# A fused attention and MLP kernel on one core: the order of every engine planned by a list scheduler, and later scores computed on two 64-row TensorE tiles

## The chip, the cores and the metric

The kernel runs on 1 core of a Trainium2 chip. The time is the device time of one execution in microseconds (us), taken as a median over runs. The engines are written as the profile names them: PE is TensorE (PEld is its weight load, which overlaps), DVE is VectorE, ACT is ScalarE, POOL is GpSimd, SP is SyncE. "The profile" is one recorded execution. Its span is the time from the first to the last instruction, 1.7 to 1.9 us shorter than the device time. Of the kernel before, one execution in three of the four groups was slow (345.9, 345.4 and 346.0 us); the medians and ranges below contain it, the ratios leave it out.

## The reference

Block-sparse attention, then a residual MLP with token mixing. The inputs are 4 batches, 8 heads, 768 tokens and 64 dimensions a head; the MLP is 512 wide with 2048 hidden units.

```python
scores = (q @ k.T) / 8                      # per batch and head, 768 x 768
scores = where(mask, scores, -1e9)          # 32x32 blocks: window, first and last, 3 sampled ones
attn   = softmax(scores);  x = attn @ v     # heads side by side: x is 768 x 512 per batch
a1 = alpha1 * x + beta1
u  = x + lam * (w_tok @ a1)                 # token mixing, 768 x 768
a2 = alpha2 * u + beta2
out = u + lam * (relu(a2 @ w_ch1) @ w_ch2)  # 512 -> 2048 -> 512
```

The q and k inputs are normal draws times 0.1, so all scores are close to 0.

## The kernel before

Heads are taken in 16 pairs. A pair's 2 x 768 x 768 transposed scores are cut into 9 units of 1024 columns. For each unit, PE makes the scores into one of two score buffers (`sps`, two PSUM banks each), ACT takes the exp into `eT` (float16), and PE multiplies that with v (PV). The mask rides in the contraction: 64 rows of q and k plus 24 rows that hold the block mask.

```python
def emit_qk(b, n, u):
    sps = ps.tile([P, UN], FP, name="sps", tag="sps", bufs=2)
    ...
        nc.tensor.matmul(sps[:, ...w columns],
            kx[h][0:KC, ts(jt, P)],          # KC = 64 + 24 rows: k and block indicator
            qx[h][0:KC, c : c + w], ...)     # q and mask bias
    eT = wk.tile([P, UN], F16, name="eT", tag="eT", bufs=5)
    nc.scalar.activation(eT[:], sps[:], AF.Exp, bias=EXPB, scale=SCALE)
```

The order of instructions is set by hand, by a loop over the 144 units. Each step issues the scores of unit i, the PV matmuls of unit i-2, one piece of token mixing, and as many MLP matmuls as a "credit" in estimated nanoseconds allows. The engines keep that order.

```python
for i in range(len(units) + LAG):
    emit_qk(b, n, u)
    ...                                      # loads, casts, transposes at fixed steps
    credit += work[ph] / NS
    if i >= NS: spent += filler(C1 if i % 2 else C2)     # MLP groups
    if i >= LAG: ... pv_tile(...)                         # PV of unit i - 2
    if mixq: spent += mix_next(i)                         # token mixing
    if i >= NS: spent += filler(1e9)
```

PSUM: two score buffers, two general banks (`mm`), one bank for PV (`ops`), one for the second MLP product (`cp`). From pair 7 on, q and k are transposed by DMA instead of PE. The MLP of a batch can start only when all four pairs of that batch have been mixed, so batch 0 has no MLP work to fill PE with.

The softmax here doesn't subtract the row's maximum and nothing guards it: scores larger than these inputs give would overflow.

## Time and profile before

| | before |
|---|---|
| device time, median (range), 3 executions | 342.8 us (340.6 to 345.9) |
| span | 339.7 us |
| PE, DVE, ACT busy | 319.1, 177.7, 192.0 us |
| first MLP matmul | 72.0 us |

First the page. Its part 1 gives each engine's busy time with its share of the span and its instruction count; part 2 gives the busy tenths in 40 slices, with the granted PE clock and the load of the DMA engines; part 4 is the chain of waits by engine.

```profile
PE 319.1 (94%) x3216; PEld 205.9 (61%) x3248; DVE 177.7 (52%) x359; ACT 192.0 (57%) x230; POOL 45.0 (13%) x71
...
PE   6898988689989999999999999999999999999995
...
DVE  4399989577774646365544545364543727100011
...
PEclk9799999899999999999999999999999999999999
DMA  7999999614292949295954525252420021000011
...
PE 80%; DVE 13%; issue 3%; DMA 2%; ACT 1%; POOL 0%; ACTq 0%; DVEq 0%; POOLq 0%
```

PE is the chain. The weak part is the first quarter, where DVE and the DMA engines are full. The windows view shows the same per 20 us. Its columns are the stretch, its length, the busy time of PE, PEld, DVE, ACT and POOL (with instruction counts), the clock, the DMA share and GB/s.

```profile
20.00:40.00 20.00, 18.19 (x283) 14.48 (x281) 18.74 (x41) 17.16 (x18) 11.73 (x18) 1.00 1.15 234
40.00:60.00 20.00, 17.40 (x260) 13.38 (x259) 17.71 (x45) 14.34 (x16) 7.13 (x11) 1.00 1.27 204
60.00:80.00 20.00, 16.50 (x241) 12.43 (x242) 12.88 (x29) 10.34 (x12) 1.41 (x2) 0.91 0.30 44
...
160.00:180.00 20.00, 19.89 (x196) 12.72 (x197) 9.98 (x20) 11.60 (x14) 2.86 (x4) 1.00 0.64 107
```

"Busy" overstates PE, because the recorded durations of successive matmuls overlap: a 512-column one lasts some 384 ns, and the next starts 216 ns after it. What counts is the distance from start to start. In the timeline of PE (start, length, operation, count) one score unit runs from 162.61 to 163.05, so 1024 columns take 0.44 us; four 384-column matmuls take 0.65 us.

```profile
161.72 0.41 PE L357 MATMUL ops<-vext,eT 128*128 128x65 f16 x8
161.96 0.81 PE L454 MATMUL mm<-uT,w1b 128*128 128x384 bf16 x4
162.61 0.60 PE L336 MATMUL sps<-qx,kx 88*128 88x512 bf16 x3
```

The measured spacings (56 ns for 128 columns, 109 for 256, 162 for 384, 216 for 512, about 30 for 65) lie on a line, 0.417 ns a column plus 2.5, with a floor for short ones (25 ns for 1 column). Whatever a distance has beyond that line is called a gap below; time lost to a slower clock counts as a gap too. "PE work" is the sum of spacings over all matmuls. For this kernel it is 308.2 us. (32 of its 3248 matmul records are missing from the trace; the sum counts them, and the 6 us that they take are not counted as gaps.)

### The profile page before, as it was taken

The numbers are of one execution on the slowest core, as the hardware profiler recorded it, in microseconds if no ns is written. First come the engines' busy times: TensorE is split into PE (matmuls) and PEld (weight loads), VectorE is DVE, ScalarE is ACT, GpSimd is POOL, SyncE is SP. The second block draws the span as 40 slices with busy tenths as digits, with TensorE's granted clock in tenths as the row PEclk, the third lists the DMA queues.
The fourth block names the chain that finished last, engine by engine and source line by source line (L and its number), as shares of the span: only waits on it lengthen the run. The fifth ranks groups of instructions, "written<-read, shape, count | busy, mean of one in ns | idle before, by whom it ended". The sixth has DMA issues, their size and how long they took to land.

```text
span 339.7 us, 7549 instructions
## 1 busy us (share of the span) xinstructions
PE 319.1 (94%) x3216; PEld 205.9 (61%) x3248; DVE 177.7 (52%) x359; ACT 192.0 (57%) x230; POOL 45.0 (13%) x71
## 2 busy tenths in 40 slices
PE   6898988689989999999999999999999999999995
PEld 3586766567665757566566756567566655555542
DVE  4399989577774646365544545364543727100011
ACT  5698786365756565566556564475656550373420
POOL 7466332101201111010100000000000000000000
PEclk9799999899999999999999999999999999999999
DMA  7999999614292949295954525252420021000011
GB/s 155 192 254 221 206 207 202 91 25 59 42 136 46 162 89 172 57 132 62 154 87 76 72 56 125 56 94 54 79 71 32 2 56 62 33 31 31 33 62 62
DMA packets 57685, 32.61 MB, mean 96 GB/s; under 512 B 38924, under 2 KB 53428, under 8 KB 57652
## 3 DMA queue, kind: packets, MB, share of 16 engines
q0 software_dynamic: 15984, 15.47, 28.9%
q1 hardware_dynamic: 41344, 16.42, 23.2%
q8 instruction: 25, 0.41, 0.5%
q10 hardware_dynamic: 324, 0.23, 0.2%
q14 instruction: 8, 0.07, 0.1%
HBM read 30.90 MB, written 6.29 MB: 109 GB/s over the span
## 4 chain that ended last, share of the span: by engine, by line
PE 80%; DVE 13%; issue 3%; DMA 2%; ACT 1%; POOL 0%; ACTq 0%; DVEq 0%; POOLq 0%
PE cp L486 21%; PE mm L454 19%; PE sps L336 14%; PE mm L409 8%; PE ops L357 8%; PE sps L454 3%; PE ops L486 3%; DMA v<-in_v_dram 2%; DVE a1p L396 2%; DVE x_sb L374 2%; DVE ot L495 1%; DVE x_sb L420 1%; DVE kx L297 1%; DVE ub L421 1%; DVE qx L296 1%
## 5 line engine op out<-in xcount | busy, mean ns | idle before, releaser
L345 ACT ACTIVATE eT<-sps 128x1024 f16<-128x1024 f32 x144 | 145.8, 1024 | 87.9 <-PE sps L336 87.2
L454 PE MATMUL mm<-uT,w1b 128*128 128x384 bf16 x444 | 88.3, 325 | 2.0 <-ACT hts L462 1.5
L336 PE MATMUL sps<-qx,kx 88*128 88x512 bf16 (+1 forms) x384 | 87.3, 329 | 0.9 <-ACT eT L345 0.5
L486 PE MATMUL cp<-w2b,hts 128*128 128x512 bf16 x308 | 79.9, 378 | 2.7 <-DVE ot L495 1.0
L357 PEld LDWEIGHTS <-eT 128*128 128x128 f16 x1152 | 53.9, 98 | 28.5 <-DVE x_sb L374 5.2
L454 PEld LDWEIGHTS <-w1b 128*128 128x128 bf16 x512 | 47.9, 97 | 34.5 <-issue 2.5
L486 PEld LDWEIGHTS <-hts 128*128 128x128 bf16 x384 | 36.3, 97 | 37.3 <-issue 2.5
L357 PE MATMUL ops<-vext,eT 128*128 128x65 f16 x1008 | 52.4, 195 | 3.9 <-DVE x_sb L374 2.4
L462 ACT ACTIVATE hts<-mm,b1t 128x384 bf16<-128x384 f32 x64 | 37.1, 579 | 33.1 <-PE mm L454 31.8
L466 DVE TENSOR_SCALAR hts<-mm,b1t 128x384 bf16<-128x384 f32 x47 | 28.9, 615 | 40.3 <-PE mm L454 34.4
L336 PEld LDWEIGHTS <-kx 88*128 88x128 bf16 x384 | 32.5, 98 | 14.5 <-issue 0.7
L409 PE MATMUL mm<-a1p,wtokT 128*128 128x128 bf16 x576 | 39.3, 219 | 1.4 <-DVE kx L297 1.1
L495 DVE TENSOR_TENSOR ot<-x_sb,cp 128x512 f32<-128x512 f32 x21 | 14.4, 685 | 44.4 <-PE cp L486 44.2
L409 PEld LDWEIGHTS <-wtokT 128*128 128x128 bf16 x576 | 33.1, 98 | 2.5 <-DVE kx L297 1.2
L420 DVE TENSOR_TENSOR x_sb<-x_sb,mm 128x384 f32<-128x384 f32 (+1 forms) x35 | 18.1, 518 | 24.8 <-PE mm L409 24.4
L185 POOL DMA_DIRECT2D v<-in_v_dram x16 | 11.6, 723 | 84.4 <-DVE vext L320 70.9
L421 DVE TENSOR_TENSOR ub<-x_sb,a_bc 128x384 bf16<-128x384 f32 (+1 forms) x35 | 18.3, 523 | 1.2
L374 DVE TENSOR_TENSOR x_sb<-ops,rcp 128x384 f32<-128x384 f32 x28 | 15.6, 557 | 1.0
L399 DVE TENSOR_TENSOR a1p<-a1p,b_bc 128x768 bf16<-128x768 bf16 x16 | 15.3, 957 | 0.6
L396 DVE TENSOR_TENSOR a1p<-x_sb,a_bc 128x768 bf16<-128x768 f32 x16 | 15.3, 956 | 0.5
L462 ACT ACTIVATE hts<-sps,b1t 128x384 bf16<-128x384 f32 x17 | 9.9, 581 | 9.1 <-PE sps L454 8.6
L185 POOL DMA_DIRECT2D q<-in_q_dram x15 | 10.8, 717 | 32.3 <-DVE relp L288 12.4
(77 smaller groups left out, 155.9 us busy)
## 6 DMA issues: line engine op xcount, KB each, us to landing
out_dram<-ot SPq DMA_DIRECT2D x24, 256.0 KB, 2.0
v<-in_v_dram POOLq DMA_DIRECT2D x16, 192.0 KB, 6.0
q<-in_q_dram POOLq DMA_DIRECT2D x15, 192.0 KB, 6.2
k<-in_k_dram POOLq DMA_DIRECT2D x15, 192.0 KB, 6.5
w1b<-in_moe_w_ch_dram POOLq DMA_DIRECT2D x4, 512.0 KB, 9.9
w2b<-in_moe_w_ch_dram POOLq DMA_DIRECT2D x4, 512.0 KB, 15.2
wtk<-in_moe_w_tok_dram POOLq DMA_DIRECT2D x3, 384.0 KB, 9.6
a_bc<-in_moe_alpha_dram POOLq DMA_DIRECT2D x2, 256.0 KB, 7.9
```

Of the source, the lines that this page charges most:

```text
L185: nc.gpsimd.dma_start(t[:], pair_ap(src, b, n))
L336: nc.tensor.matmul(sps[:, f - u * UN : f - u * UN + w], kx[h][0:KC, ts(jt, P)], qx[h][0:KC, c : c + w], start=True, stop=True,)
L345: nc.scalar.activation(eT[:], sps[:], AF.Exp, bias=EXPB, scale=SCALE)
L357: nc.tensor.matmul(ops[(b, n, a)][:, t * VW : t * VW + D + 1], eTs[(b, n, u)][:, ts(c, P)], vx[:, a, jt, 0 : D + 1], start=(r == 0), stop= ...
L374: nc.vector.tensor_tensor(out=x_sb[:, s0 : s0 + NT, h * D : (h + 1) * D], in0=op[:, :, 0:D], in1=rcp[:].unsqueeze(2).broadcast_to([P, NT, D]),
L396: nc.vector.tensor_tensor(out=a1p[:], in0=x_sb[:, s0 : s0 + NT, cs], in1=bc(a1_bc, NT), op=ALU.mult)
L409: nc.tensor.matmul(tp[:, j, :], wtokT[:, s, ts(m * g + j, P)], a1p[:, s, :], start=(s == 0), stop=(s == NT - 1),)
L421: nc.vector.tensor_tensor(out=ub[:, gs, :], in0=sl, in1=bc(a2_bc, m), op=ALU.mult)
L454: nc.tensor.matmul(hp[:, 0:HS], w1b[:, dk, ts(f, P)], uTs[b][:, dk, ts(hf, HS)], start=(dk == 0), stop=(dk == 3),)
L462: nc.scalar.activation(hts[k][:, f, :], hp[:, 0:HS], AF.Relu, bias=b1t[:, f : f + 1], scale=1.0)
L466: nc.vector.tensor_scalar(out=hts[k][:, f, :], in0=hp[:, 0:HS], scalar1=b1t[:, f : f + 1], scalar2=0.0, op0=ALU.add, op1=ALU.max,)
L486: nc.tensor.matmul(cps[k][:], hts[k][:, nk, ts(m, P)], w2b[:, nk, :], start=(nk == 0), stop=(nk == 15),)
```

## The change

Two things were done at once.

1. A `Plan` class takes every operation with an estimated duration, its dependencies, its buffers and a "due" value, and simulates the engines inside the program. Whenever an engine is free, the ready operation with the smallest due value is emitted. Some copies and ReLUs may go to ACT or DVE, whichever takes them first. PSUM becomes two score buffers plus four general banks (`gb`), and `eT` has 7 buffers instead of 5.
2. From pair 6 on (90 of the 144 units) the scores contract over 64 rows only. Two such matmuls are issued side by side, on rows 0 to 63 and 64 to 127 of PE. The mask no longer fits in the contraction; it becomes a product of `eT` with a 0/1 mask on DVE (the mask table is made once, with 6 small exps). Each pair's q and k are transposed by three DMAs, and two DMAs issued from POOL copy q's halves to the other 64 partitions ("swap").

```diff
+class Plan:
+    def run(self):
+        t = min(self.free.values())
+        while todo:
+            ...                                # release buffers that are done at t
+                for op in todo:
+                    if any(d.vis is None or d.vis > t for d in op.deps): continue
+                    ...                        # buffers there? engine free?
+                        if self.free[e] <= t and (e not in best or op.due < best[e][0].due):
+                            best[e] = (op, o)
+                op, (e, occ, vis) = min(best.values(), key=lambda x: x[0].due)
+                ...
+                self.free[e] = t + occ
+                op.emit(op)
...
-    for i in range(len(units) + LAG):
-        ...
-            emit_qk(b, n, u)
...
+    def emit_qk_rows(pi, u, key):
+        ...
+            for r in range(2):
+                rows = slice(r * D, (r + 1) * D)
+                o = r * 512 + f % 512
+                nc.tensor.matmul(
+                    spsT[sl(key)][:, o : o + w],
+                    kd[i][rows, h, g, :],
+                    qx2[i][rows, h, c : c + w],
...
+    def emit_mult(op, i):
+        e = eTt[sl(("eT", i))][:].rearrange("p (r c) -> p r c", r=2)
+        x = i % NU * 512 % HF
+        nc.vector.tensor_tensor(out=e, in0=e, in1=msk[:, :, x : x + 512], op=ALU.mult)
...
+        batch = [i] if pi < T0 else [i, i + 1]      # T0 = 6: two tiled units in one PE group
+        occ = 437 if pi < T0 else 640
```

## The prediction

> **What bounds the kernel now.** TensorE: PE 319.1 us of a 339.7 us span (94%, the page), DVE 52%, ACT 57%; the chain of waits is 80% PE. From start to start in the timeline a matmul costs 56 ns (128 columns), 109 (256), 162 (384), 216-220 (512), about 30 (65). Times the counts that is 308 us of PE work, so only some 31 us are gaps: 7 in the first 20 us, 15 from 20 to 100, about 0.5 in each later 20, 4 after the last matmul. The windows agree: PE 16.5-18.6 of each 20 us from 20 to 100, 19.3-19.9 from 100 to 320. The early gaps come from ACT (17.2 of 20 us at 20-40) and DVE (18.7, 17.7 of 20): the MLP can start only when batch 0 is mixed; its first matmul comes at 74 us.
>
> **What changes, costed.**
> 1. Scores of pairs 6 to 15 (90 of 144 units). A unit of 1024 columns costs about 440 ns; after, two units run side by side as 64-row tiles. The Trainium skill, "TensorEngine Tiling (Array Packing)", section Key Properties, says that tiles work in parallel and that changing the tiling mode drains TensorE; no run shows either yet. Perfect overlap would be 440 ns for two; with a drain on each side (duration 384 minus spacing 220: some 165 ns, an estimate) 770. I take 640 against 880: 45 x 0.24 = 11 us less. Mask scores add 2 us, fewer transposes and warm-ups take 1.5 off. PE work: 298 us.
> 2. DVE: 90 products of 128x1024 f16; that shape costs 682 ns today (w2b x lam): +61 us. ReLUs 47 to 72 by the built order (615 ns): +15. Casts and copies: -13. DVE 178 to about 245 us, 76% of the span: not the bound, but products now lie between exp and PV.
> 3. ACT is unchanged at about 193 us.
> 4. DMA: per tiled pair three half-size transposes and two swaps through POOL replace two full ones; off the path unless a load holds POOL's queue.
> 5. The list scheduler acts mainly before 100 us (copies on ACT or DVE, 7 buffers of E, four general PSUM banks): 6-8 of the 15 us from 20 to 100 come back. Later PE has only 5 us to win, and a static order whose times differ from the chip's may lose as much. The end is full already.
>
> **Sum.** 298 us PE work + head 6.5 + early 7 + middle 6 + end 4 = 321.5 us; I lean a little lower on overlap: span 318, device time **320 us**, range **309 to 333**. Nearly all PE work saved counts, as PE is the chain from 100 us to the end. Faster by over 2%: 0.92; within 2%: 0.06; slower: 0.02.
>
> **What would show the steps.** (a) Tiled score matmuls start in pairs a few ns apart; a batch of two units takes 550-700 ns of PE; 880 means no overlap. (b) The product's mean is 650-700 ns; 1200 means it lost its fast mode. (c) First MLP matmul before 62 us; PE at 18 or more of each 20 us from 40 to 100. (d) From 100 us PE above 19 of 20; waits of PV on the product and of tiled scores on qx under 5 us in total. (e) DVE about 245 us.
>
> **What would make it wrong.** Drains larger than assumed at 90 mode changes; DVE near saturation from 60 to 240 us, so that PV, mix and ReLU come late against the plan; one batch taking both score buffers, so that exps and scores alternate; DVE work or full buffers holding POOL's transfers.

## The result, and the profile after

| | before | after |
|---|---|---|
| device time, median (range), 4 executions | 341.8 us (340.6 to 345.9; fast ones to 342.8) | 323.7 us (323.1 to 324.9) |
| ratio, 95% interval | | 0.949 (0.943 to 0.954) |
| span | 339.7 us | 323.1 us |
| PE, DVE, ACT busy | 319.1, 177.7, 192.0 us | 310.7, 229.6, 183.8 us |
| first MLP matmul | 72.0 us | 68.6 us |

A ratio here and below is the mean time of one kernel's fast runs over that of the kernel before in the same rounds, so it is not quite the ratio of the medians.

The page after the change, same lines:

```profile
PE 310.7 (96%) x3238; PEld 189.0 (58%) x3238; DVE 229.6 (71%) x430; ACT 183.8 (57%) x218; POOL 55.9 (17%) x87
...
PE   7897989899999999999999999999999999999995
...
DVE  4669976876697979796868786876768685555531
...
PEclk9999988999999999999999999999999999999999
DMA  6999999935453747374733231423020100110011
...
PE 86%; DMA 4%; ACT 4%; DVE 3%; POOL 1%; issue 1%; ACTq 0%; DVEq 0%
```

PE is still the chain, and more of it. DVE went from 52% to 71% and is not on it. The windows after:

```profile
20.00:40.00 20.00, 17.64 (x275) 13.08 (x272) 18.51 (x40) 15.70 (x18) 11.97 (x18) 1.00 1.15 228
40.00:60.00 20.00, 18.11 (x290) 13.74 (x286) 14.18 (x34) 16.20 (x18) 8.57 (x13) 0.91 1.27 203
60.00:80.00 20.00, 18.95 (x229) 12.52 (x229) 14.93 (x28) 15.59 (x19) 3.48 (x5) 1.00 0.68 109
...
160.00:180.00 20.00, 20.00 (x222) 12.08 (x220) 15.75 (x29) 12.77 (x17) 1.22 (x2) 1.00 0.29 68
```

From 60 us on PE is fuller; from 20 to 60 us it is hardly better than before. Now the tiled scores. The groups view (line, operation, tiles, shape and count, then total busy time and mean ns, then idle time before) has the new products, and the PE timeline a batch of two tiled units:

```profile
L834 DVE TENSOR_TENSOR eT<-eT,msk 128x1024 f16<-128x1024 f16 x90 | 60.9, 684 | 12.0 <-ACT eT L827 12.0
```

```profile
151.01 0.41 PE L853 MATMUL gb<-vext,eT 128*128 128x65 f16 x8
151.35 0.61 PE L817 MATMUL sps<-qx,kx 64*128 64x512 bf16 x6
151.89 1.04 PE L1193 MATMUL gb<-w2b,hts 128*128 128x512 bf16 x4
```

The six matmuls are three pairs. In the trace the two of a pair start 2 to 5 ns apart (median 3), so the tiles do overlap: two units take 0.44 us of array time instead of 0.88. But eight PV matmuls of 30 ns would end at 151.25, and the batch starts at 151.35. It holds PE until 151.89, 0.10 us longer than its 0.44. Over all batches, a 128-row matmul followed by a 64-row one is spaced 97 ns wider than usual (median), and the way back 93 ns. This fits the drain at a change of tiling mode that the Trainium skill, "TensorEngine Tiling (Array Packing)", section Key Properties, speaks of; the page gives no figure. The weight loads (PEld) fit it too: after a 384- or 512-column matmul of the same mode, the next load starts 162 ns before its matmul (median), but at all 90 changes of mode it starts only 3 to 5 ns before. So neither a load nor a matmul starts during the extra 93 to 97 ns. With both changes of mode, a batch costs about 0.63 us instead of 0.88.

The sums of PE spacings and gaps, in us, account for the whole span:

| | before | after |
|---|---|---|
| PE work | 308.2 | 290.9 |
| changes of tiling mode (45 x 0.19) | 0 | 8.6 |
| gaps before 100 us | 21.9 | 17.7 |
| gaps after 100 us | 4.1 | 0.6 |
| before the first and after the last matmul | 5.5 | 5.3 |
| sum = span | 339.7 | 323.1 |

The tiles and a few dropped matmuls saved 17.3 - 8.6 = 8.7 us, and closed gaps saved 7.7 us, half of them early and half late. That is a reading of one trace; the experiments test it.

### The profile page after: what moved, and what is told of

The parts are those of the page before. It is cut to its first block, busy times and chain, and to the rows that moved or that the text cites. A ratio compares the mean times of both kernels' runs of the same rounds, so it can differ in the third digit from the quotient of the medians.

```text
span 323.1 us, 7682 instructions
## 1 busy us (share of the span) xinstructions
PE 310.7 (96%) x3238; PEld 189.0 (58%) x3238; DVE 229.6 (71%) x430; ACT 183.8 (57%) x218; POOL 55.9 (17%) x87
## 4 chain that ended last, share of the span: by engine, by line
PE 86%; DMA 4%; ACT 4%; DVE 3%; POOL 1%; issue 1%; ACTq 0%; DVEq 0%
PE gb L1135 26%; PE gb L1193 25%; PE gb L1037 11%; PE gb L853 10%; PE sps L817 8%; PE sps L798 4%; DMA wtk<-in_moe_w_tok_dram 3%; ACT eT L827 3%; PE sps L1193 1%; PE gb L347 1%; PE sps L584 1%; DMA sampi<-in_sampled_blocks_dram 1%; DVE w2b L565 1%; ACT kx L395 0%; PE gb L539 0%
## 5 line engine op out<-in xcount | busy, mean ns | idle before, releaser
L1135 PE MATMUL gb<-uT,w1b 128*128 128x384 bf16 x512 | 99.9, 326 | 0.0
L1193 PE MATMUL gb<-w2b,hts 128*128 128x512 bf16 x368 | 92.6, 379 | 0.0
L834 DVE TENSOR_TENSOR eT<-eT,msk 128x1024 f16<-128x1024 f16 x90 | 60.9, 684 | 12.0 <-ACT eT L827 12.0
L1165 DVE TENSOR_SCALAR hts<-gb,b1t 128x384 bf16<-128x384 f32 x72 | 44.4, 617 | 29.0 <-PE gb L1135 28.2
L853 PE MATMUL gb<-vext,eT 128*128 128x65 f16 x1152 | 59.5, 194 | 5.1 <-ACT eT L827 4.8
L1157 ACT ACTIVATE hts<-gb,b1t 128x384 bf16<-128x384 f32 x56 | 32.5, 580 | 25.5 <-PE gb L1135 23.5
L1037 PE MATMUL gb<-a1p,wtokT 128*128 128x128 bf16 x576 | 36.8, 223 | 0.2 <-DVE a1p L1021 0.2
L798 PE MATMUL sps<-qx,kx 88*128 88x512 bf16 (+1 forms) x144 | 33.4, 336 | 0.0
L817 PE MATMUL sps<-qx,kx 64*128 64x512 bf16 (+1 forms) x240 | 27.3, 327 | 0.0
L1058 DVE TENSOR_TENSOR x_sb<-x_sb,gb 128x384 f32<-128x384 f32 x32 | 17.6, 550 | 13.3 <-PE gb L1037 13.3
L1065 DVE TENSOR_TENSOR ub<-x_sb,a_bc 128x384 bf16<-128x384 f32 x32 | 17.6, 553 | 0.3
L798 PEld LDWEIGHTS <-kx 88*128 88x128 bf16 x144 | 11.1, 99 | 4.2 <-issue 0.9
## 6 DMA issues: line engine op xcount, KB each, us to landing
v<-in_v_dram POOLq DMA_DIRECT2D x16, 192.0 KB, 6.5
q<-in_q_dram POOLq DMA_DIRECT2D x15, 192.0 KB, 7.3
k<-in_k_dram POOLq DMA_DIRECT2D x15, 192.0 KB, 6.6
```

Source lines behind the costliest of these rows:

```text
L798: nc.tensor.matmul(spsT[sl(key)][:, o : o + w], kx2[i][0:KC, a, ts(jt, P)], qx2[i][0:KC, a, c : c + w], start=True, stop=True,)
L817: nc.tensor.matmul(spsT[sl(key)][:, o : o + w], kd[i][rows, h, g, :], qx2[i][rows, h, c : c + w], start=True, stop=True,)
L834: nc.vector.tensor_tensor(out=e, in0=e, in1=msk[:, :, x : x + 512], op=ALU.mult)
L853: nc.tensor.matmul(bk[:, t * VW : t * VW + D + 1], eTt[sl(("eT", i))][:, ts(col, P)], vx[:, a, jt, 0 : D + 1], start=(r == 0), stop=(r >= ...
L1037: nc.tensor.matmul(tp[:, j, :], wtokT[:, s, ts(m * g + j, P)], a1p[sl(ak)][:, s, :], start=(s == 0), stop=(s == NT - 1),)
L1058: nc.vector.tensor_tensor(out=s, in0=s, in1=tp, op=ALU.add)
```

## The experiments

Twelve kernels ran, in three groups. The kernel before ran beside each group (medians 342.4, 342.0 and 341.9 us). The changed kernel did not; differences from it below compare its median of 323.7 us across groups.

### 1. Tiled scores over all 128 rows

The order on every engine is the same as in the changed kernel; only the row range differs, so the scores are wrong. (The comparison with the reference passed all the same: with scores so close to 0, it does not see them.)

```diff
-                rows = slice(r * D, (r + 1) * D)
+                rows = slice(0, P)
```

> The changed kernel in the same order on every engine, but each of the 240 later score matmuls runs over all 128 rows instead of 64 (wrong result on purpose): no overlap in pairs and no change of tiling mode. Theory (the tiles save array time that lies on the path): a batch of two units takes 880 ns of PE instead of the measured 630, 45 x 0.25 = 11 us more, about 335 us. Rival (PE is not what ends the middle of the kernel; DVE with its products is): within 2 us of 323.7.

Measured: 333.4 us, ratio 0.973 (0.966 to 0.979), 9.7 us slower than the changed kernel; 11 were expected. Its PE timeline:

```profile
151.13 0.41 PE L853 MATMUL gb<-vext,eT 128*128 128x65 f16 x8
151.38 1.03 PE L817 MATMUL sps<-qx,kx 128*128 128x256 bf16 x6
152.24 0.41 PE L853 MATMUL gb<-vext,eT 128*128 128x65 f16 x8
```

The same six matmuls now hold PE for 0.86 us, with no extra time before or after. PE time saved by the tiles is time saved by the kernel; the rival, that DVE sets the pace there, falls.

### 2. One tiled unit at a time

```diff
-        batch = [i] if pi < T0 else [i, i + 1]
+        batch = [i]
-        occ = 437 if pi < T0 else 640
+        occ = 437 if pi < T0 else 417
```

> Later scores issued one unit at a time instead of two: 90 entries into and exits from the 64-row mode instead of 45. Theory (each entry and exit costs 95 ns, as the gaps in the trace show): 45 x 0.19 = 8.5 us more, about 332 us. Rival (one batch taking both score buffers makes exps and scores alternate and costs time): no slower than 324 us, perhaps faster.

Measured: 332.7 us, ratio 0.971 (0.965 to 0.977), 9.0 us slower than the changed kernel; 8.5 were expected from 45 more pairs of mode changes. (The plan was made anew, so the order differs too. The trace has 85 entries into the 64-row mode, 40 more than before and not 45, and the extra spacing at its changes sums to 8.1 us more than in the changed kernel. The other 0.9 us are not accounted for.) In the timeline a lone unit starts 0.10 us late and ends 0.10 us late as well:

```profile
150.02 0.42 PE L853 MATMUL gb<-vext,eT 128*128 128x65 f16 x8
150.37 0.39 PE L817 MATMUL sps<-qx,kx 64*128 64x512 bf16 x2
150.69 1.04 PE L1193 MATMUL gb<-w2b,hts 128*128 128x512 bf16 x4
```

Batches that take both score buffers did no harm. A tiled unit on its own costs 0.22 + 0.19 = 0.41 us, next to 0.44 untiled, so nearly all of the tiles' gain comes from batching: this run is no faster than run 4 below, which has no tiles.

### 3. Without the products

```diff
-        nc.vector.tensor_tensor(out=e, in0=e, in1=msk[:, :, x : x + 512], op=ALU.mult)
+        pass
```

> The changed kernel in the same order with the 90 mask products left out (wrong result on purpose: later pairs are not masked). DVE loses 61 us of busy time. Theory (the products are hidden behind PE): 0 to 2 us faster. Rival (the products sit on the path between exp and PV, or hold other DVE work back): 5 us or more faster.

Measured: 323.8 us, ratio 0.946 (0.940 to 0.952); the result is wrong. Taking 61 us of work off DVE gains nothing, so in this order the products are hidden.

### 4. The scheduler alone

All scores stay untiled, with the mask in the contraction and the DMA transposes of the kernel before from pair 7 on, all written as operations of the new plan. This is not one of the two kernels with a line changed; the parts that matter:

```diff
-T0 = 6
+T0 = NP            # no pair is tiled
+DMA_FROM = 7
...
+    def prep_dma(pi):    # as before: cast into rel, one DMA transpose each for q and k
```

> The list scheduler alone: the kernel before's operations (all scores on 128 rows with the mask in the contraction, transposes by DMA from pair 7 on, no products) ordered by the new scheduler. Theory (half of the gain is gaps closed by the order): PE work 307.5 us plus gaps as in the changed kernel without its mode changes (18 us) plus 5 us at the ends, span 331, about 332 us. Rival (the gain is the tiling): about 341 us.

Measured: 332.2 us, ratio 0.971 (0.965 to 0.977): 10.2 us faster than the kernel before, and 8.5 us slower than the changed kernel. The sums of its trace: PE work 308.3 us, gaps 18.2 us before 100 us and 0.4 us after. So the scheduler closed 7.4 us of gaps (26.0 to 18.6) at unchanged PE work, and the tiles add the rest. The 10.2 us is more than 7.4, which goes along with the clock: the executions of the kernel before in this group had mean clocks of 0.977 to 1.000, those of this run 0.984 to 1.000, and at a clock of 1.000 the two took 339.5 and 331.9 us, 7.6 us apart. The two halves of the change are about equal. Tiles under the order of the kernel before were not run, so whether the halves would add in either sequence is not shown. Nor does this run part the order from the buffers that came with it (7 of `eT`, four general banks).

### 5 to 7. Why the gaps from 20 to 60 us stayed

I had expected the scheduler's gain there, and the gaps stayed at 8.4 us (8.2 before). The weights' DMA was one suspect: its share is over 1 in both windows. The other was how PE and ACT hand work to each other. The PE timeline of the changed kernel, with idle time and what ended it in brackets:

```profile
25.08 0.60 PE L798 MATMUL sps<-qx,kx 88*128 88x512 bf16 x3
26.91 0.42 PE L853 MATMUL gb<-vext,eT 128*128 128x65 f16 x8 [1.23 <-ACT eT L827]
...
28.94 0.42 PE L853 MATMUL gb<-vext,eT 128*128 128x65 f16 x8 [0.26 <-ACT eT L827]
29.19 2.17 PE L1037 MATMUL gb<-a1p,wtokT 128*128 128x128 bf16 x36
31.20 0.60 PE L798 MATMUL sps<-qx,kx 88*128 88x512 bf16 x3
```

ACT's side of the same stretch:

```profile
25.01 0.80 ACT L395 COPY kx<-gb 64x768 bf16<-64x768 bf16 x1 [0.24 <-DVE qx L397]
25.83 3.97 ACT L827 ACTIVATE eT<-sps 128x1024 f16<-128x1024 f32 x4
31.90 2.85 ACT L827 ACTIVATE eT<-sps 128x1024 f16<-128x1024 f32 x3 [2.10 <-PE sps L798]
```

At 25 us a copy out of PSUM, which the plan let ACT take, holds up an exp, and PE waits 1.23 us for that exp. At 29 us PE does both halves of a pair's token mixing in one go, and ACT waits 2.10 us for scores. One waits for the other in turn, and neither gets the time back. Three edits: copies on DVE alone; scores due two units earlier; and both, with the two halves of token mixing moved apart.

```diff
# run 5 (three places: q and k, w_tok, uT)
-                    pl.both(("qkc", pi, a, j), dve(768, 2), act(768), ...
+                    pl.dve(("qkc", pi, a, j), dve(768, 2), ...
# run 6
-            i,           # due of a score group
+            i - 2,
# run 7: both, and (likewise for the two DVE operations that follow each half)
-                dd + 1 + g,         # due of half g of token mixing
+                dd + 1 + 2 * g,
```

> The changed kernel with the copies out of PSUM (q and k, w_tok, uT) allowed on VectorE alone; in the changed kernel the scheduler puts 7 of them (0.8 us each) on ScalarE among the early exps. Theory (before 62 us PE waits for exps, 4.3 us in all, because these copies and long PE groups hold the exps up): 1 to 3 us faster than 323.5 and less idle PE from 20 to 60 us. Rival (the early PE gaps come from the weights' DMA, whose engines are full until 64 us): within 1 us of 323.5.

> The changed kernel with the scores given an urgency two units earlier, so that PE refills the score buffers before token mixing and transposes. Theory (PE and ScalarE hold each other up early, since a PE group of 2.2 us starves the exps and then PE waits for one): 2 to 4 us faster, first MLP matmul before 66 us instead of 68.6. Rival (early gaps come from the DMA): within 1 us of 323.5.

> Both edits, and the two halves of a pair's token mixing given urgencies two units apart instead of one. Theory: 4 to 6 us faster than the changed kernel, 317.5 to 319.5 us, PE gaps from 20 to 60 us falling from 8.4 to 3 to 5 us. Rival (DMA): within 1 us of 323.5.

| run | median | ratio, 95% interval | against the changed kernel | first MLP matmul |
|---|---|---|---|---|
| 5 copies on DVE | 320.3 us | 0.936 (0.933 to 0.940) | -3.4 us | 63.6 us |
| 6 scores earlier | 319.9 us | 0.936 (0.932 to 0.940) | -3.8 us | 63.8 us |
| 7 all three | 316.6 us | 0.927 (0.922 to 0.932) | -7.1 us | 63.7 us |

All three gain, at the same loads and the same DMA load (share 1.14 or 1.15 and 1.27 in the two windows), so the DMA was not what held PE for most of it: the PE gaps from 20 to 60 us fell from 8.4 to about 5, 4 and 2.5 us. Run 6 gained what was expected; runs 5 and 7 gained a little more. (The profiled execution of run 7 was its slowest, 319.8 us; its first 20 us hold 127 matmuls, against 161 to 174 in the profiles of the changed kernel and of runs 5, 6 and 12, so its first MLP matmul is late for this kernel.)

At most a small part of it is the clock. In the changed kernel's window from 40 to 60 us the granted clock averages 0.91, and one group of 36 mixing matmuls that takes 2.17 us elsewhere takes 3.29:

```profile
47.90 3.29 PE L1037 MATMUL gb<-a1p,wtokT 128*128 128x128 bf16 x36
```

The longest wait that PE shows in that trace is the 1.23 us above. The Trainium skill, "TensorE: Matmul & The Clock Gate", section A second HAM failure mode: psum-queue depth-cycling, says that many short idle times of PE can also make the clock swing. This trace fits that, with one fall to half clock of 3.4 us; what made it fall was not tested. A mean clock of 0.995 over 323 us is at most 1.6 us of the 7 us. In runs 5 to 7 the mean is 0.997 to 1.000. One execution of the changed kernel had a mean clock of 1.000 and still took 323.1 us; against it the three edits gain 2.8, 3.2 and 6.5 us.

### 8 to 11. Tiling two more pairs

If PE work is what counts, tiling pairs 4 and 5 too should give 3.6 us more.

```diff
-T0 = 6
+T0 = 4
```

> The changed kernel with tiled scores from pair 4 on instead of pair 6: 9 batches and 24 PE transposes more or less, 9 x 0.25 + 24 x 0.056 = 3.6 us less PE work. Theory A (PE work counts everywhere): 320 us. Theory B (batch 0's stage and the start of batch 1 are held by ScalarE and VectorE, and the products, mask and DMA transposes come into the stretch where VectorE and the DMA engines are fullest): within 1.5 us of 323.5.

Measured: 332.1 us, ratio 0.971 (0.967 to 0.976). That is 8.4 us slower than the changed kernel, worse than either theory. Its windows show PE at about half clock for long:

```profile
40.00:60.00 20.00, 19.10 (x194) 12.21 (x192) 8.09 (x19) 12.22 (x15) 6.96 (x10) 0.59 1.29 192
60.00:80.00 20.00, 16.62 (x178) 11.57 (x176) 15.88 (x30) 11.65 (x12) 4.12 (x6) 0.73 0.82 118
```

I took the clock for the cause and put dummy matmuls into that stretch, two or one before each mask score group and each score unit from 24 to 35. They write into a score buffer that is overwritten at once; the order is otherwise the same.

```diff
+                    for w in range(2):          # run 10: range(1)
+                        nc.tensor.matmul(
+                            spsT[sl(key)][:, w * 512 : w * 512 + 512],
+                            warm[:, 0:P], warm[:, 0:512], start=True, stop=True)
```

> The slow version with tiles from pair 4 (332.1 us), the same order on every engine, plus 36 dummy 512-column matmuls on PE between 30 and 60 us (two before each mask score group and each score unit 24 to 35; they are overwritten). Theory (that version is slow because PE is thinly used from 40 to 63 us and its clock drops to half, 0.59 and 0.73 in two stretches of 20 us): the clock stays above 0.9 there and, though 36 x 0.216 = 7.8 us of PE work is added, the time falls to 322 to 329 us. Rival (the stretch is held by ScalarE's extra mask exps and late transposes, the clock only follows): 332 us or more.

> The same with 18 dummy matmuls, one in each place, 3.9 us of PE work. Theory: if one is enough to hold the clock, 320 to 327 us; if the clock still drops, about 332. Rival: 332 us or more at any clock.

Measured: 331.4 us, ratio 0.970 (0.965 to 0.974), and 331.2 us, ratio 0.970 (0.964 to 0.975). The dummies did hold the clock: 1.00 from 40 to 60 us in both, though it still fell to 0.74 from 60 to 80 in run 10. The time did not move. The theory of the clock falls: the slow clock sits in a stretch that is waiting for something else.

> The best version so far (316.6 us: copies on VectorE alone, scores two units earlier, mixing halves apart) with tiles from pair 4 on. PE work falls by 9 x 0.25 + 24 x 0.056 = 3.6 us. Theory A (denser PE work keeps the clock): 313 to 316 us. Theory B (mask exps, products and DMA transposes in the fullest stretch cost more than the tiles save): 318 to 330 us, with a lower clock before 80 us.

Measured: 334.7 us, ratio 0.979 (0.974 to 0.984), 18 us slower than run 7, which differs from it only in T0. This run shows what is waited for, because its early stage is quick: PE reaches the tiled scores at 58 us and stops.

```profile
57.12 0.92 PE L852 MATMUL gb<-vext,eT 128*128 128x65 f16 x16
67.88 1.28 PE L816 MATMUL sps<-qx,kx 64*128 64x512 bf16 x6 [9.84 <-DMA qx<-qx]
```

The chain of waits before it (start, length, what):

```profile
36.62 19.84 DMA w2b<-in_moe_w_ch_dram
...
57.13 10.71 DMA qx<-qx
```

The first tiled pair needs the swap of q's halves, a DMA of 96 KB issued from POOL. By this chain POOL issued it 0.67 us after a load of the second MLP weight had landed, which is taken for what it waited for, and the swap then took 10.71 us to land. In the changed kernel, where the first tiled scores start at 86 us, the swaps land in 2.4 us (median); the plan assumed 3.3. From 40 to 60 us the DMA engines are full (share 1.29 or more in runs 8 and 11). In runs 8 to 11 the first tiled unit's exp starts at 65.7, 65.7, 65.0 and 68.8 us, however quickly or slowly PE came to it: PE waited 0.4, 0, 3.8 and 9.8 us for the swap. The Trainium skill, "DMA: Bandwidth & Descriptors", section Issuing engines are not separate DMA queues, says that DMAs from all issuing engines run on the same 16 DMA engines and interleave; the swap's landing time fits that. How the delay divides between POOL's late issue and the slow landing was not tested apart.

The wait of 9.84 us is only half of run 11's 18 us. The clock has a part here: it was 0.81 from 40 to 60 us and 0.59 from 60 to 80 us, which loses 12 us of full clock in all. In the wait itself, from 58.04 to 67.88 us, it was 0.57, which loses 4 us that PE could not use anyway. The other 8 us, an estimate from these figures, came on top, before and after the wait. So in runs 8 to 10 the clock did not set when the tiled scores began, but a low clock is not free where PE has work.

So with T0 = 4 PE waits for a swap that comes late behind weights and loads, which keep the DMA engines busy until about 64 us. T0 = 5 was not run, and whether an earlier swap, or loading the weights later, would make T0 = 4 pay stays open.

### 12. A wider distance

```diff
# against run 7; likewise for the two DVE operations that follow each half
-                dd + 1 + 2 * g,
+                dd + 1 + 3 * g,
```

> The best version so far with the halves of token mixing three units apart instead of two. Expected within 1.5 us of 316.6: its PE gaps from 20 to 60 us are 2.5 us in all, so there is little left to win.

Measured: 316.4 us, ratio 0.926 (0.922 to 0.931), the same as run 7. Run 7 and this one beat both kernels; against the changed kernel they are about 2.2% faster by the medians, though the two did not run beside each other. The windows of run 12, early stage:

```profile
20.00:40.00 20.00, 19.61 (x308) 15.86 (x305) 18.71 (x41) 17.11 (x19) 11.73 (x17) 1.00 1.14 227
40.00:60.00 20.00, 19.74 (x369) 16.57 (x367) 19.55 (x45) 15.76 (x17) 8.66 (x12) 1.00 1.27 203
```

PE is busy 19.6 and 19.7 us of 20 here, where it was 17.6 and 18.1, and its first MLP matmul starts at 60.4 us. Gaps from 20 to 100 us, mode changes included, fell from 11.8 us to 5.0 us. The loads are the same and the DMA share is 1.14 and 1.27, as in the changed kernel.

## Why the prediction was right, and where its steps were not

The time was predicted as 320 us with a range of 309 to 333, and 323.7 was measured. Point by point:

- **PE is the bound, and nearly all PE work saved counts.** Right from 100 us on: run 1 puts the saved work back and loses 9.7 us. Run 8 shows where it is not so: work saved ahead of 65 us is worth nothing if a DMA is late.
- **Tiles: 640 ns a batch instead of 880, 11 us.** Right. The batch costs about 0.63 us, and runs 1 and 2 price the overlap and the mode changes apart. The PE work of 298 us was 299.5 with the mode changes. Leaning "a little lower on overlap" (from 321.5 of span to 318) was wrong; the plain sum was nearer to the measured 323.1.
- **DVE about 245 us, hidden.** The products took 684 ns each, as predicted (682). DVE came to 229.6 us, because casts, copies and the rest fell by 16 us where I took off 13, and because records that overlap count once, which hides 9 us more than before. That it is hidden is shown by run 3.
- **ACT 193 us.** It came to 183.8 us. Nothing rested on it.
- **"6-8 of the 15 us from 20 to 100 come back", and "Later PE has only 5 us to win, and a static order ... may lose as much".** Mis-sized both ways. The early gaps fell by 3 us only (14.9 to 11.8, of which some 0.8 are mode changes), while the late gaps fell from 4.1 to 0.6 us. The four gap terms of the prediction add to 23.5 us, and 23.6 us was measured (17.7 + 0.6 + 5.3): from 20 to 100 us it was 4 us short, after 100 us over 5 us too many. That the two cancel is luck, so the time came out right for a partly wrong reason.
- **First MLP matmul before 62 us.** Wrong: 68.6 us. The step behind it, that a list scheduler closes the early gaps, failed. The plan let copies and long mixing groups go ahead of exps and scores, so PE and ACT waited for each other in turn. Runs 5 to 7 show it: three edits to engine choice and due values brought 7 us. (The prediction's 74 us for the kernel before is also a misreading; its trace has 72.0.)
- **PE at 18 or more of 20 us from 40 to 100, above 19 from 100.** Right (18.1, 19.0, 20.0, then 20.0). **Waits of PV on the product and of tiled scores on qx under 5 us.** Right: the products held PE's weight loads for 2.4 us, and the swaps cost PE nothing.
- **"DMA ... off the path".** Right for T0 = 6. Runs 8 to 11 show how near it was: two pairs earlier, the same swap is the path.

## What to carry to other kernels

Price a tiling of PE as overlap minus mode changes, and batch tiled matmuls until the changes are paid: here two units a batch gained 0.25 us, and one alone gained almost nothing. A scheduler inside the program is only as good as its urgencies and its engine choice: look in the trace for two engines that wait for each other in turn, and put the feeding operation (here scores before mixing, exps before copies) first. When a clock drops, ask what PE was waiting for before you try to warm it: in runs 9 and 10 holding the clock up gained nothing while a 96 KB DMA was late.

## What the Trainium skill lacked or had wrong

- "TensorEngine Tiling (Array Packing)" says that a change of tiling mode drains TensorE, but not what it costs. Here it cost 97 ns into the 64-row mode and 93 ns out of it, and run 2, with 40 more pairs of changes, took 9.0 us more. Nor does that page say that a weight load is not started ahead across a change: here it led its matmul by 3 to 5 ns, against 162 ns within a mode. Its table gives up to 2x for a factor of 2; two units in one batch came to 0.88 / 0.63 = 1.4x, since the changes of mode take away a part of the 0.88 / 0.44 = 2x.
- "TensorE: Matmul & The Clock Gate" gives, in section Why this matters for your kernels, a rule that PE gaps must stay under about 3 us. In the changed kernel the clock fell (0.91 from 40 to 60 us) with no wait of PE over 1.3 us. The page's second failure mode covers such a case, but neither part says how thin the use of PE has to be.
- "DMA: Bandwidth & Descriptors" says that DMAs of all issuing engines interleave, but gives no time for a small one in a full stretch. A 96 KB copy within SBUF landed in 2.4 us (median) after 71 us and in 10.7 us at 57 us, when loads filled the engines.
